# Routing attention with a feed-forward block: one pair's loads ahead of the staging loads, one pair's ordering a step later, and the first result product ahead of the last hidden product

## The chip, the cores and the metric

One core of a Trainium2 chip runs the whole program. Times are device microseconds (us) of one execution; the figure compared is the median over the runs shown. The core's engines work side by side, each on its own queue of instructions: TensorE (PE, matrix products), VectorE (DVE), ScalarE (ACT), GpSimd (POOL) and SyncE (SP). SP does no arithmetic here; it issues nearly all plain DMA transfers. POOL issues the indirect ones.

## The reference

Inputs are random float32. First comes attention by clusters for 4 batches of 8 heads, 768 tokens of 64 features, 16 centroids for each head:

```python
q_assign = np.argmax(np.einsum('bhsd,hcd->bhsc', q_n, c_n), axis=-1)
k_assign = np.argmax(np.einsum('bhsd,hcd->bhsc', k_n, c_n), axis=-1)
mask = q_assign[:, :, :, None] == k_assign[:, :, None, :]
scores = scale * np.matmul(q, k.transpose(0, 1, 3, 2))
scores = np.where(mask, scores, -1000000000.0)
attn = softmax(scores)
x = (attn @ v).transpose(0, 2, 1, 3).reshape(3072, 512)
h = x @ w_in                                       # w_in 512 x 2048
g = np.maximum(h, 0.0) + alpha * np.minimum(h, 0.0)
out = g @ w_out                                    # w_out 2048 x 512
```

(`q_n`, `k_n`, `c_n` are the rows divided by their norms; the softmax is shortened here.) A query meets only the keys that have the same nearest centroid.

## The kernel before, in words

**Pairs and steps.** Two heads of one batch make a pair; there are 16. Pairs 0 to 8 are computed with a mask over all keys. Pairs 9 to 15, the seven ordered pairs, have their tokens sorted by cluster first, so that a block of queries meets only a near window of keys. The program is a hand-written order over 75 steps `u`, of which an ordered pair takes three. Pair 9 starts at step 48 (438.5 us), pair 10 at 51 (461.4), pair 11 at 54 (494.6), pair 8 in two halves at 57 and 60 (517.4, 544.2), pair 12 at 63 (575.9), 13 at 66 (621.4), 14 at 69 (661.4), 15 at 72 (702.9). After step 75 (747) only the feed-forward block of the last batch is left. A step has five slots; small pieces of preparation are listed under (step, slot), and `feed` puts feed-forward pieces of earlier batches between them: first layer L1066 on PE, its copy L1072 on ACT, its slopes L1058 on DVE, second layer L1084 on PE, additions L1090 and L1092, store L1095. Each engine works strictly in the order of its queue. So an instruction that waits holds back whatever stands behind it on that engine.

**How a pair is ordered.** `load(n)` reads q and k (L127). `order_features` transposes them on DVE (L567), `order_sims` multiplies with the centroids on PE (L575), an argmax on DVE follows in pieces (L404 to L412), then a transpose L584 and a scan L589 that counts members. `order_begins` sums counts on PE (L601); `order_ranks` and `order_rows` (L609 to L622) make of it the row to which each token goes. After that 24 indirect DMAs on POOL scatter the tokens into scratch memory (L675). They are fed from staging tiles: `order_stage` (L661) issues three SP loads (q, k, v; "a staging trio" below) into one of two tiles, and waits until the scatters that still read that tile are done. POOL is paced by ACT (L651, L652), so that scatters go out a few to a slot.

**How an ordered pair is loaded and used.** `order_load` (L681 to L708) reads the sorted rows back with 12 SP transfers: two at L688 (where each row came from), eight of 96 KB at L697 (q and k), two at L706 (v). `order_blocks` transposes q and k (two L713 on DVE), `order_queries` makes the query clusters (L719), `score` multiplies (L784; the near windows of the second half bank wait for the first exponential, L802), L825 masks, L835 and L867 add up, L873 and L881 turn and sum for the denominators, L894 folds these sums on PE, and L939 or L972 multiplies with v. Results are put back into token order by indirect transfers (L1011), fetched (L1023) and turned (L1030).

**When these happen.** Two lists of steps set it. `ORDERS` (L1369) gives the step at which `load(n)` of the n-th ordered pair is called; its features come one step later, its sims two. `order_load` is called a number of steps ahead of the pair's start (L1380):

```python
    ORDERS = [26, 29, 35, 38, 41, 56, 59]
    load_at.setdefault(u - (3 if n in (NO + 1, NO + 2, NP - 1) else 4), []).append(
        lambda n=n: order_load(n))
```

Here `u` is the first step of the pair, `NO` is 9 and `NP` is 16: pairs 10, 11 and 15 are loaded three steps ahead, the others four. What is called in `load_at` stands at the head of its step, staging trios and scatters stand in its slots.

**The last batch.** Its feed-forward block (`last_pieces`, L1142) forms 2 x 2 block products with seven multiplications instead of eight, in both layers. `hidden(x)` for x = 0 to 7 makes the products p1, p5, p2, p6, p3, p7 and p4 of the first layer (L1244, two float32 matmuls of 384 columns each); p4 of one x is held in the list `late` and run within the next. p4 is written to the PSUM bank that p7 has used, which DVE reads for an addition (L1179); slopes are at L1184. `final(t)` makes the same seven of the second layer (L1300, one float32 matmul of 256 columns for each of the eight x). For these DVE forms sums of hidden values (`g_sums`, L1223) and of the weights w_out (`w_out_sums`, L1232), four each for every x. `room_for_y` (L1338) stands between the last `hidden` and the first `final`: it runs the held p4 of x = 7, and makes the sums of x = 6 and 7.

Of the kernel before, what the change touches and what calls it, by code (L numbers as in the profile page):

```python
# [16 lines left out]
ALU = mybir.AluOpType  # L17
# [6 lines left out]
def kernel(  # L24
# [80 lines left out]
    NO = WHOLE * NCH - 3  # L105
    NP = len(pairs)
# [4 lines left out]
    def load(n):  # L111

        b, hp = pairs[n]
        for w, src in enumerate((q, k)):
            raw = inp.tile([P, 2, NJ, D], FP32, name="qk")
            if n < NCH:
                nc.sync.dma_start(
                    out=raw.rearrange("p h j d -> p h (j d)"),  # L120
                    in_=src[b, 2 * hp:2 * hp + 2].rearrange("h (p j) d -> p h (j d)",
                                                            j=NJ))
            for h in range(2):
                rows = src[b, 2 * hp + h]
                for x in range(D // Q if n >= NCH else 0):
                    r = h * D + x * Q
                    nc.sync.dma_start(  # L127
                        out=raw.rearrange("p h j d -> p (h j d)")[r:r + Q, :].rearrange(
                            "p (t i) -> p t i", i=Q),
                        in_=rows[:, x * Q:(x + 1) * Q].rearrange("(t p) i -> p t i", p=Q))  # L130
            raw_qk[n, w] = raw
# [306 lines left out]
    def prep_clusters(n):  # L438


        first = firsts.pop(n)
        ps = misc()
        for g in range(NG):
            nc.tensor.matmul(out=ps[:, g * 2 * NX:(g + 1) * 2 * NX], lhsT=spread[:, g, :],
                             rhs=first, start=True, stop=True)
        every = fsp.tile([P, NG, GT, NG, 2], BF16, name="every")
        everys[n] = every
        later(1, lambda: nc.scalar.copy(every.rearrange("p g i r h -> p (g i r h)"),
                                        ps[:, 0:NG * 2 * NX]))
        later(2, lambda: prep_keys(n))  # L450
# [114 lines left out]
    def order_features(n, w):  # L565
        us[n, w] = raw_qk.pop((n, w)).rearrange("p h j d -> p (h j d)")
        nc.vector.transpose(out=us[n, w], in_=us[n, w])  # L567

    def order_sims(n):
        hp = pairs[n][1]  # L570
        ps = misc()
        for g in range(NG):
            w, half = divmod(g, 2)
            tokens = us[n, w].rearrange("p (x g i) -> p g x i", g=2, i=Q)
            nc.tensor.matmul(out=ps[g * W:(g + 1) * W, 0:HS],  # L575
                             lhsT=cT[:, hp * W:(hp + 1) * W], rhs=tokens[:, half],
                             start=True, stop=True)
        later(1, lambda: order_counts(n, ps))
# [131 lines left out]
    def order_blocks(n, w):  # L710
        if w == 0:
            qkTs[n] = qkp.tile([P, NB * P], FP32, name="qkT")
        nc.vector.transpose(  # L713
            out=qkTs[n][:, w * S:(w + 1) * S],
            in_=raw_qk.pop((n, w)).rearrange("p h j d -> p (h j d)"))
# [170 lines left out]
    parts, totals = {}, {}  # L886
# [222 lines left out]
    KH, NQ, HC = NCH // 2, NF // 2, DM // 2  # L1109
# [32 lines left out]
    def last_pieces():  # L1142
# [53 lines left out]
        def g_sum(x, m):  # L1196

            if m == "S4":
                return s4[x]
            t = by_pair[x // 2].rearrange("p (x m q) -> p x m q", x=2, m=2)  # L1200
            return t[:, x % 2, ("S1", "S2").index(m)]
# [8 lines left out]
        def w_out_form(m, x):  # L1210
            if m in ("11", "21", "22"):
                c0 = HC * (m == "22")
                return w_out_sb[:, x if m == "11" else NQ + x, c0:c0 + HC]
            i = ("T1", "T2", "T3", "T4").index(m)
            f = x + NQ * (i // 2)
            return w_in_sb[:, KH * (i % 2):KH * (i % 2 + 1), f * P:(f + 1) * P]

        def g_sums(x):
            (t0, t1), (z0, z1) = g[x][0], g[NQ + x][0]
            S1, S2, S4 = (g_sum(x, m) for m in ("S1", "S2", "S4"))  # L1220
            for to, p, q, op in ((S1, t1, z1, ALU.add), (S2, S1, t0, ALU.subtract),
                                 (t1, t0, t1, ALU.subtract), (S4, z0, S2, ALU.subtract)):
                nc.vector.tensor_tensor(out=to, in0=p, in1=q, op=op)  # L1223

        def w_out_sums(x):

            T1, T2, T3, T4 = (w_out_form(m, x) for m in ("T1", "T2", "T3", "T4"))
            B11, B12, B21, B22 = (
                w_out_sb[:, f, c0:c0 + HC].rearrange("p (a w) -> p a w", a=KH)
                for f in (x, NQ + x) for c0 in (0, HC))  # L1230
            for to, p, q in ((T1, B12, B11), (T2, B22, T1), (T3, B22, B12), (T4, B21, T2)):
                nc.vector.tensor_tensor(out=to, in0=p, in1=q, op=ALU.subtract)  # L1232

        late = deque()
# [101 lines left out]
            return [p1, p5, p6, p2, p7, p3, p4]  # L1336

        def room_for_y():  # L1338
            late.popleft()()
            t = sorts["xmore"].tile([P, NCH, HS], FP32, name="xT").rearrange(  # L1340
                "p c q -> p (c q)")
            ys.extend(ypool.tile([P, DM], FP32, name="y") for _ in range(HJ))
            ys.extend(t[:, i * DM:(i + 1) * DM] for i in range(HJ))
            for x in (NQ - 2, NQ - 1):
                g_sums(x)
            for x in (NQ - 2, NQ - 1):
                w_out_sums(x)
        pieces = []
        for x in range(NQ):
            pieces += hidden(x)  # L1350
        pieces.append(room_for_y)
        for t in range(HJ):
            pieces += final(t)
# [12 lines left out]
    FREE = SLOTS * SB - 3  # L1366


    ORDERS = [26, 29, 35, 38, 41, 56, 59]  # L1369
    prep_at, load_at = {}, {}  # L1370
    for (n, half), u in start_of.items():
        def at(step, slot, piece):
            prep_at.setdefault((step, slot), []).append(piece)
        if half is None:
            t = ORDERS[n - NO]
            load_at.setdefault(t, []).append(lambda n=n: load(n))
            for i in range(2):
                at(t + 1, FIRST + i, lambda n=n, i=i: order_features(n, i))
            at(t + 2, 2, lambda n=n: order_sims(n))
            load_at.setdefault(u - (3 if n in (NO + 1, NO + 2, NP - 1) else 4), []).append(  # L1380
                lambda n=n: order_load(n))
            at(u - 4, 0, lambda n=n: prep_clusters(n))
            for i in range(2):
                at(u - 1, i, lambda n=n, i=i: order_blocks(n, i))
                at(u - 1, FIRST + i, lambda n=n, i=i: order_queries(n, i))
            continue
        if half == 0:
            if n < NCH:
                if n > 1:
                    load_at.setdefault(max(u - 7, 0), []).append(lambda n=n: load(n))  # L1390
                if n > 0:
                    load_at.setdefault(max(u - 6, 0), []).append(lambda n=n: load_v(n))
            else:
                load_at.setdefault(u - 9, []).append(lambda n=n: load(n))
                load_at.setdefault(u - 7, []).append(lambda n=n: load_v(n))
            if n < NCH:
                for g in range(len(groups)):
                    at(u - 4, FIRST + g, lambda n=n, g=g: prep_features(n, g))
            else:
                for w in range(2):  # L1400
                    at(u - 7, FIRST + w + (u - 7 == TOGETHER - 1),
                       lambda n=n, w=w: prep_blocks(n, w))
            at(u - (3 if n < NCH else 5 if u - 6 < TOGETHER else 6), FIRST,
               lambda n=n: prep_sims(n)) if u - 6 < 2 * TOGETHER else at(
                   u - 6, FIRST + 1, lambda n=n: prep_sims(n))
            if n >= NCH:
                at(u - 4, FIRST if u - 4 < TOGETHER else 0, lambda n=n: prep_clusters(n))
        if n < NCH:

            if half == 1 or n == 0:  # L1410
                at(u - (3 if half else 1), FIRST,
                   lambda n=n, half=half: prep_queries(n, half, 0))
            continue
        for h in range(2):
            at(u - 1, FIRST + h, lambda n=n, half=half, h=h: prep_queries(n, half, h))
# [44 lines left out]
    for u in range(-AHEAD, TOGETHER):  # L1460
        for piece in load_at.get(u, []):
            piece()
        n, half, s = steps[max(u, 0)]
# [51 lines left out]
    for u in range(TOGETHER, NS + 1):  # L1515
        for piece in load_at.get(u, []):
            piece()
        if u < NS:
            n, half, s = steps[u]
# [107 lines left out]
    for i in (1, 3):  # L1627
# [14 lines left out]
                            op=ALU.subtract)  # L1642
    nc.vector.tensor_tensor(out=ends[:, 1, :], in0=ends[:, 1, :], in1=spans[:, 2, :],
                            op=ALU.subtract)
# [172 lines left out]
```

## Time and profile before

| | us |
|---|---|
| median of three runs | 940.79 (940.7 to 941.31) |
| profiled execution | 941.51 |
| its span on the core | 939.6 |
| PE busy | 919.1 |
| VectorE busy | 656.2 |
| POOL busy | 382.3 |
| ScalarE busy | 262.8 |

The span runs from the first to the last instruction on the core; the profiled execution's own time lies 1.9 us above it. Busy time is the sum of an engine's instructions, waits not counted. The mean granted clock of PE was 0.997 of full speed. Lines such as L713 are those of the kernel before. In a timeline row the columns are start, duration, engine, line, operation, output and inputs, shapes and count; a bracket at its end gives the time for which the engine stood idle before it, and what ended that. The trace counts two PE instructions for each float32 matmul of the code, and the text counts as the trace does. Rows of one line are joined, so the duration of an "x8" row is from the start of the first to the end of the last, with up to 0.2 us of overlap with its neighbours.

### The profile page before, as it was taken

The page shows a single profiled execution, that of the slowest core. Times are in us where ns is not written, and L with a number is a line of the kernel's source. Part 1 is how long each engine was busy: PE and PEld are TensorE (multiplying, and loading weights), DVE is VectorE, ACT ScalarE, POOL GpSimd, SP SyncE. Part 2 cuts the span into 40 slices and gives each one's busy share as a digit, 9 for nine tenths or more (in the row PEclk, how much of TensorE's full clock was granted, in tenths as well). Part 3 has the DMA queues.
Part 4 walks back from the last instruction along what each step waited for, and adds up shares of the span by engine and source line. Part 5 has one row for each costly group of instructions (what it writes and reads, how often), then busy time and mean ns, then how long its engine had stood idle before and what let it go on. Part 6 is the DMA issues. An engine that isn't in the chain of part 4 may idle for free.

```text
span 939.6 us, 11988 instructions
## 1 busy us (share of the span) xinstructions
PE 919.1 (98%) x3963; PEld 495.3 (53%) x3963; DVE 656.2 (70%) x1246; ACT 262.8 (28%) x661; POOL 382.3 (41%) x580
## 2 busy tenths in 40 slices
PE   8999999999999999999999999999999999999997
PEld 5534444445455454454544544555555555556886
DVE  5797798799679589598987889754647135598100
ACT  5764444323023132231212332122212120221000
POOL 2333222200026677478575786668533471000000
PEclk9999999999999999999999999999999999999999
DMA  8433758039002635252952383662501012000000
GB/s 298 135 117 98 144 131 150 18 62 196 1 9 72 156 82 137 62 120 76 176 100 41 59 138 73 149 124 60 92 31 27 12 37 53 1 0 1 23 23 25
DMA packets 226708, 77.71 MB, mean 83 GB/s; under 512 B 210752, under 2 KB 214544, under 8 KB 226640
## 3 DMA queue, kind: packets, MB, share of 16 engines
q1 hardware_dynamic: 217728, 62.72, 30.9%
q0 software_dynamic: 8064, 13.78, 4.7%
q8 instruction: 33, 0.54, 0.2%
q10 hardware_dynamic: 848, 0.39, 0.2%
q14 instruction: 35, 0.29, 0.1%
HBM read 52.25 MB, written 24.25 MB: 81 GB/s over the span
## 4 chain that ended last, share of the span: by engine, by line
PE 82%; DVE 10%; SPq 3%; DMA 1%; issue 1%; POOL 1%; ACT 1%; DVEq 0%; POOLq 0%; ACTq 0%
PE fps L1084 24%; PE fps L1066 22%; PE sps L784 6%; PE vps L939 5%; PE sps L1244 4%; PE sps L1300 4%; PE vps L1244 2%; PE vps L1300 2%; PE fps L784 2%; SPq L697 1%; PE mps L972 1%; PE fps L1300 1%; PE fps L1244 1%; PE vps L972 1%; SPq L127 1%
## 5 line engine op out<-in xcount | busy, mean ns | idle before, releaser
L1066 PE MATMUL fps<-xT,w_in_sb 128*128 128x384 f32 x768 | 258.9, 490 | 0.0
L1084 PE MATMUL fps<-w_out_sb,gT 128*128 128x512 f32 x576 | 254.8, 596 | 2.5 <-DVE gT L1058 2.5
L675 POOL DMA_INDIRECT scratch<-stage,off x168 | 177.9, 1059 | 75.1 <-issue 29.6
L1066 PEld LDWEIGHTS fps<-xT,w_in_sb 128*128 128x128 f32 x768 | 142.5, 190 | 103.1 <-issue 4.3
L1084 PEld LDWEIGHTS fps<-w_out_sb,gT 128*128 128x128 f32 x576 | 107.4, 190 | 134.8 <-issue 121.4
L1072 ACT COPY gT<-fps 128x384 f32<-128x384 f32 x96 | 46.0, 479 | 236.2 <-PE fps L1066 236.2
L652 POOL COPY paced<-pace 1x1 f32<-1x1 f32 x205 | 51.2, 250 | 139.5 <-ACT pace L651 138.9
L1058 DVE SCALAR_TENSOR_TENSOR gT<-gT,alpha 128x384 f32<-128x384 f32 x96 | 61.2, 647 | 58.7 <-ACT gT L1072 58.5
L1011 POOL DMA_INDIRECT back<-rows,off x84 | 85.7, 1021 | 24.2 <-issue 18.6
L784 PE MATMUL sps<-qkT 64*128 64x384 f32 (+1 forms) x464 | 86.1, 490 | 0.4 <-DVE qkT L713 0.4
L805 ACT ACTIVATE E<-sps 128x768 f32<-128x768 f32 (+1 forms) x76 | 56.3, 786 | 62.6 <-PE sps L793 38.4
L784 PEld LDWEIGHTS sps<-qkT 64*128 64x128 f32 x464 | 41.8, 188 | 39.7 <-issue 14.6
L825 DVE SCALAR_TENSOR_TENSOR more<-aq,key,more 128x384 f32<-128x384 bf16 (+2 forms) x116 | 60.4, 577 | 0.0
L939 PE MATMUL vps<-E,vt 128*64 128x384 f32 x292 | 54.2, 495 | 1.5 <-DVE xT L1042 1.5
L271 POOL TENSOR_TENSOR w_in_sb<-w_in_sb,power 128x512 f32<-128x512 f32 x16 | 25.7, 1612 | 68.6 <-DVE w_in_sb L268 68.6
L825 DVE SCALAR_TENSOR_TENSOR E<-aq,key,E 128x384 f32<-128x384 bf16 (+2 forms) x88 | 45.3, 569 | 0.6 <-ACT E L802 0.6
L271 POOL TENSOR_TENSOR w_out_sb<-w_out_sb,power 128x512 f32<-128x512 f32 x16 | 22.5, 1412 | 56.0 <-DVE w_out_sb L268 56.0
L907 DVE RECIPROCAL inverses<-mps 64x12 f32<-64x12 f32 (+1 forms) x42 | 10.5, 249 | 48.1 <-PE mps L894 47.9
L835 DVE TENSOR_TENSOR acc<-acc,E 128x768 f32<-128x768 f32 x35 | 33.3, 951 | 14.6 <-ACT E L805 13.6
L1090 ACT COPY y<-fps 128x512 f32<-128x512 f32 x18 | 10.6, 587 | 102.3 <-PE fps L1084 102.3
L1092 DVE TENSOR_TENSOR y<-y,fps 128x512 f32<-128x512 f32 x24 | 16.3, 680 | 28.5 <-PE fps L1084 28.5
L805 ACT ACTIVATE more<-sps 128x768 f32<-128x768 f32 (+1 forms) x40 | 29.2, 764 | 12.5 <-PE sps L784 11.6
(284 smaller groups left out, 1178.4 us busy)
## 6 DMA issues: line engine op xcount, KB each, us to landing
raw<-in_moe_w_in_dram SPq DMA_DIRECT2D x16, 512.0 KB
raw<-in_moe_w_out_dram SPq DMA_DIRECT2D x16, 512.0 KB
out_dram<-y SPq DMA_DIRECT2D x21, 256.0 KB
qk<-scratch SPq DMA_DIRECT2D x56, 96.0 KB
qk<-in_q_dram SPq DMA_DIRECT2D x48, 96.0 KB
qk<-in_k_dram SPq DMA_DIRECT2D x48, 96.0 KB
w_in_kept<-w_in_sb SPq DMA_DIRECT2D x8, 512.0 KB
vt<-in_v_dram SPq DMA_DIRECT2D x9, 384.0 KB
```

The lines of the kernel that those rows point to most:

```text
L652: nc.gpsimd.tensor_copy(out=sorts["paced"], in_=token)
L675: nc.gpsimd.indirect_dma_start(out=scratch[n][1][h * NX + xx], out_offset=bass.IndirectOffsetOnAxis(ap=ranks[n][:, xx, h:h + 1], axis=0), ...
L784: nc.tensor.matmul(out=bank(ps, h, m), lhsT=qkT[r:r + D, S + c * P:S + (c + 1) * P], rhs=qkT[r:r + D, tokens], start=True, stop=not early_ ...
L805: nc.scalar.activation(out=E[:, :, 0:m], in_=ps[:, :, 0:m], func=AF.Exp, scale=SCALE)
L825: nc.vector.scalar_tensor_tensor(out=e, in0=of, scalar=keys[n][:, NJ + c, h:h + 1], in1=e, op0=ALU.is_equal, op1=ALU.mult)
L939: nc.tensor.matmul(out=po[r:r + D, 0:HS], lhsT=vts[n][:, h, c, :], rhs=e[:, h, :], start=(c == 0), stop=(c == NJ - 1))
L1011: nc.gpsimd.indirect_dma_start(out=to[i], out_offset=bass.IndirectOffsetOnAxis(ap=place[:, h, j:j + 1], axis=0), in_=rows[j // HJ][:, j % ...
L1058: nc.vector.scalar_tensor_tensor(out=gs[f], in0=gs[f], scalar=alpha[:, f:f + 1], in1=gs[f], op0=ALU.mult, op1=ALU.max)
L1066: nc.tensor.matmul(out=ps[:, 0:HS], lhsT=w_in_sb[:, c, f * P:(f + 1) * P], rhs=xTs[b, half][:, c, :], start=(c == 0), stop=(c == NCH - 1))
L1084: nc.tensor.matmul(out=ps[:, 0:DM], lhsT=gs[f][:, i * P:(i + 1) * P], rhs=w_out_sb[:, f, :], start=on and f == f0, stop=off and f == f0 + ...
L1244: nc.tensor.matmul(out=bank[to], lhsT=w_in_form(m, x, cc), rhs=rhs[:, cc, :], start=start and cc == 0, stop=cc == KH - 1, skip_group_check ...
L1300: nc.tensor.matmul(out=bank[to], lhsT=g_form(m, x, t), rhs=w_out_form(n, x), start=start and x == 0, stop=x == NQ - 1, skip_group_check=no ...
```

## The change

Three edits. First, the leads of `order_load` become a list, in which pair 11 has 4 steps instead of 3: its loads are called at step 50, not 51. All other leads keep their value. Second, the last entry of `ORDERS` is 60, not 59: loading, ordering, staging and scattering of pair 15 start one step later. Third, `room_for_y` no longer runs the held p4 of x = 7 and no longer makes the sums itself. It appends them to `late`, as eight pieces: piece i of x = 6, then piece i of x = 7, for i = 0 to 3, each with one sum of hidden values and one of weights. `late` is emptied in p1 of `final(0)`, which was there before: p1 is issued first, then p4 of x = 7, then the sums.

```diff
-        def g_sums(x):
+        def g_sums(x, parts=range(4)):
             (t0, t1), (z0, z1) = g[x][0], g[NQ + x][0]
             S1, S2, S4 = (g_sum(x, m) for m in ("S1", "S2", "S4"))
-            for to, p, q, op in ((S1, t1, z1, ALU.add), (S2, S1, t0, ALU.subtract),
-                                 (t1, t0, t1, ALU.subtract), (S4, z0, S2, ALU.subtract)):
+            sums = ((S1, t1, z1, ALU.add), (S2, S1, t0, ALU.subtract),
+                    (t1, t0, t1, ALU.subtract), (S4, z0, S2, ALU.subtract))
+            for to, p, q, op in [sums[i] for i in parts]:
                 nc.vector.tensor_tensor(out=to, in0=p, in1=q, op=op)
 
-        def w_out_sums(x):
+        def w_out_sums(x, parts=range(4)):
...
-            for to, p, q in ((T1, B12, B11), (T2, B22, T1), (T3, B22, B12), (T4, B21, T2)):
+            sums = ((T1, B12, B11), (T2, B22, T1), (T3, B22, B12), (T4, B21, T2))
+            for to, p, q in [sums[i] for i in parts]:
                 nc.vector.tensor_tensor(out=to, in0=p, in1=q, op=ALU.subtract)
...
         def room_for_y():
-            late.popleft()()
...
-            for x in (NQ - 2, NQ - 1):
-                g_sums(x)
-            for x in (NQ - 2, NQ - 1):
-                w_out_sums(x)
+            late.extend(lambda i=i, x=x: (g_sums(x, [i]), w_out_sums(x, [i]))
+                        for i in range(4) for x in (NQ - 2, NQ - 1))
...
-    ORDERS = [26, 29, 35, 38, 41, 56, 59]
+    ORDERS = [26, 29, 35, 38, 41, 56, 60]
+    LEADS = [4, 3, 4, 4, 4, 4, 3]
...
-            load_at.setdefault(u - (3 if n in (NO + 1, NO + 2, NP - 1) else 4), []).append(
+            load_at.setdefault(u - LEADS[n - NO], []).append(
                 lambda n=n: order_load(n))
```

## The prediction, made before the result was known

> **What bounds the kernel now.** First the engine totals. TensorE (PE) is busy for 919.1 of 939.6 us and no other engine is above 70%, so time can be won only where PE waits or runs slowly.
>
> ```profile
> span 939.6 us, 11988 instructions
> PE 919.1 (98%) x3963; PEld 495.3 (53%) x3963; DVE 656.2 (70%) x1246; ACT 262.8 (28%) x661; POOL 382.3 (41%) x580
> ```
>
> Second, the waits of PE over the whole run. A row is: waiting line, releaser, us in total, times, longest. Those the change can reach:
>
> ```profile
> PE fps L1084 <- DVE gT L1058: 2.5, 2, 2.3
> PE mps L575 <- issue: 1.3, 1, 1.3
> PE mps L601 <- DVE simT L589: 1.1, 2, 0.8
> PE fps L784 <- ACT E L802: 0.7, 1, 0.7
> PE sps L1244 <- DVE gT L1179: 0.6, 1, 0.6
> PE sps L784 <- DVE qkT L713: 0.4, 1, 0.4
> ```
>
> Third, the chain of waits around the largest of them, at 490 us. A row is start, duration, what:
>
> ```profile
> 486.40 3.60 DMA qk<-scratch
> ...
> 490.13 0.98 DVE qkT L713
> ...
> 491.53 0.54 DVE gT L1058
> ...
> 492.11 2.59 PE fps L1084 x4
> 494.70 2.26 PE sps L784 x8
> ```
>
> PE waits for a slope (L1058). The slope stands on VectorE (DVE) behind the second transpose L713 of pair 11, and that one waits for the last load of pair 11. Fourth, the timeline of SyncE's queue (SP) shows why the load is late (start, us, instruction):
>
> ```profile
> 466.33 0.39 SPq L141 DMA_DIRECT2D vt<-in_v_dram  x1
> 472.92 0.61 SPq L661 DMA_DIRECT2D stage<-in_q_dram  x1
> ...
> 479.09 0.60 SPq L661 DMA_DIRECT2D stage<-in_q_dram  x1
> ...
> 482.36 4.61 SPq L697 DMA_DIRECT2D qk<-scratch  x8
> ```
>
> SP stood still twice, 466.7 to 472.92 and 474.95 to 479.09, in front of a staging load that waits for the scatters still reading its tile. The loads L697 stood behind both. Last, windows of 1 us over PE (busy, busy with count, granted clock, DMA share, GB/s):
>
> ```profile
> 491.00:492.00 1.00, 0.00 (x0) 1.00 0.00 0
> ...
> 494.00:495.00 1.00, 1.00 (x3) 0.50 0.00 0
> ...
> 497.00:498.00 1.00, 1.00 (x8) 1.00 0.12 33
> ```
>
> The clock was halved from about 493.3 to 496.8. So the wait costs more than its 2.29 us.
>
> **What the Trainium skill says.** "TensorE: Matmul & The Clock Gate", Part 1: the clock has two values, full and half; it drops after an idle window of about 3.4 us and comes back after about as long of work. The trace agrees on one half and on the length (493.3 to 496.8), but here an idle of 2.29 us was enough, while PE's other idles of 1.0 to 1.5 us show no drop; the trace decides. "DMA: Bandwidth & Descriptors", section on the anatomy of one DMA: transfers wait on nothing, the issuing sequencer does, before it dispatches. SP's two stops above are that, so the place in SP's order is what matters. "PSUM — Partial Sum Buffer", section on bank collisions: PE must not write a bank while it is read. This is the 0.65 us wait of part C.
>
> **Part A: pair 11's load one step earlier (step 51 to 50).** In the built program its 12 DMAs (2 at L688, 8 at L697, 2 at L706) now stand directly behind the store L1095 of 465.68, ahead of L141 and both staging trios. They can go: the last scatter of pair 11 was issued at 414.91, and the buffer's last reader, pair 10's second L713, ended near 460. They issue over 466.3 to 473.4 (7.1 us, the old length from 481.06 to 488.4), 15 us earlier. DVE's order is the same. Its first L713 lost 1.44 us and its second 1.80 us to these loads. Without them DVE starts the first at 485.85 and runs two L713 at 0.98, L455, L459 (0.4 together) and the first slope (0.5) to about 488.65. PE ends its 12 matmuls L1084 at 489.82 and finds the slope ready, 1.2 us early. So the wait of 2.29 goes. So does the halved clock: x4 of L1084 take 1.72 instead of 2.59 (a group of 16 takes 6.87 undisturbed), and the 8 score matmuls L784 take 1.29 instead of 2.26 (same form at 461.40 and 575.94). The fold L894 then starts at 489.82+1.72+1.29+0.54 = 493.4 instead of 497.5: **4.1 us**.
> What is pushed back: L141 and the first trio by about 1 us (SP is done with the loads at 473.4, the trio began at 472.92); the second trio still waits for its scatters until about 479.1. The scatters fed by them may come 1 to 2 us later; the scatter queue (POOL) later has 6.63 us of wait for its pace at 495.54, which covers this. DMA load between 466 and 472 is light (44 to 55 GB/s).
>
> **Part B: ordering of pair 15 one step later (59 to 60).** What moves: on SP the four-plus-four loads L127 (548.90 to 554.5) go behind a staging trio; on DVE two L567, then the argmax (L404 to L412), L584, L589 and ranks; on PE the sims L575 and the begins L601; on SP and POOL pair 15's staging trios and scatters.
>
> ```profile
> 560.35 1.07 PE L575 MATMUL mps<-qk,cT 128*32 128x384 f32 x8 [1.34 <-issue]
> 575.94 1.29 PE L784 MATMUL sps<-qkT 64*128 64x224 f32 x8 [0.40 <-DVE qkT L713]
> 578.47 0.80 PE L784 MATMUL fps<-qkT 64*128 64x320 f32 x2 [0.71 <-ACT E L802]
> 586.22 0.58 PE L601 MATMUL mps<-simT,row 128*128 128x1 f32 x4 [0.83 <-DVE simT L589]
> ```
>
> L575 waits for the second L567, which waited 2.23 and 0.33 us for its loads. In the built order L575 stands in the middle of the second group of L1084, about 569 us; L567 can be done at about 565.6: 1.34 goes. Pair 12's second L713 no longer has L404, L405 and L406 of pair 15 in front of it (some 1.7 us of DVE): done about 571.7, wanted at 574.0: 0.40 goes. L601 stands behind 8 L1084 and 12 L1066, its scan has 8 us more: 0.83 goes. The 0.71 stays: it is the second half bank waiting for the first exponential, in both programs. Sum **2.57 us**. Thin place: L404 now stands in front of the parts that the fold L894 of pair 12 needs, behind a transpose L1030 that may wait for a fetch; worked out, 576.4 against 577.2 wanted, 0.8 us to spare. Bounds for B: below, -1 us (that margin overrun, nothing else gained in this stretch); above, 3.3 (the 0.71 goes too). Later price: pair 15's order_load, issued from 657.01 to 663.9 and landed by about 666, now comes about one step later, 13 us (pair 13 to pair 14 is 40 us for three steps), while PE is 6.7 earlier by then. Pair 15's first L713 starts at about 692, so of 26 us of slack some 6 are left: cost nothing, but less cover than before.
>
> **Part C: first product of the results ahead of the last of the first layer.** Nothing is added or removed; DVE has as many sums as before.
>
> ```profile
> 857.81 1.45 PE L1244 MATMUL sps<-xT,w_in_sb 128*128 128x384 f32 x4
> 859.91 1.56 PE L1244 MATMUL sps<-vt,w_in_sb 128*128 128x384 f32 x4 [0.65 <-DVE gT L1179]
> 868.22 3.77 PE L1300 MATMUL vps<-w_in_sb,qkT 128*128 128x256 f32 x16
> ```
>
> Product p4 waits for the addition of p7 (859.30 + 0.56), which reads p4's bank. After: p7 ends 859.26, p1 takes 3.45 in between, p4 1.29, then p2, p5, p6 at 3.45 each: 874.35, where before the product after p6 began at 875.27. Gain **0.9 us** (0.65, the 0.12 by which p4 ran long, and 0.15 in p5, whose sums came late). Needed: p1's slopes (done 860.37, wanted by 862.3), the slopes behind p4 (865.1, wanted 867.0), the first sums interleaved (867.7, wanted 870.5). Bounds: 0 if a sum in the new order is late by as much, 1.2 at most.
>
> **Sum.** 4.1 + 2.57 + 0.9 = 7.6 us. The profiled execution took 941.51 (span 939.6 and 1.9 around it), so 933.9; the median of the runs is 940.79, 0.72 lower, so **933.2**. From 730 to 857 PE has no wait that takes any of it back; between 595 and 730 the gaps that remain belong to PE's own order.
>
> **Rivals.** (1) A and C hold, B does not: DVE is the bound of the stretch from 560 to 590 (it is busy there without a gap), and L404 ahead of the fold's input turns the 0.8 us margin into a wait of the size removed. For it: a thin margin, and L1030 waiting on a fetch. Against: 2 us of argmax work leave the place. 940.79 - 5.0 = 935.8. (2) B and C hold, A does not: the slope has to wait for something else, such as a delayed load or a later staging trio, and PE idles again at 490. Against: the loads have 15 us. About 937.3 with the clock drop kept. (3) The wait goes but the halved clock turns up at another place, since the window that decides it runs freely; 2 of 7.6 us are clock: 935.5. (4) Nothing measurable, the next late input stands right behind each: 940 to 941. (5) Slower: pair 15's later staging. Its 24 scatters go out at the pace that ScalarE sets; if order_load(15) slips, L713 at step 71 and the score at step 72 wait, 1 us for each, plus 1.8 us of halved clock. It decides from a slip of some 12 us beyond the 13 worked out: 6 to use up the slack, about 6 more and the 1.8 to lose the gain. 941 to 946.
>
> **How the numbers follow.** All parts hold: 0.68, with 931 to 935 (clock and small idles). Rival 1: 0.11; rival 2: 0.08; rival 3: 0.05; rival 4: 0.04; rival 5: 0.04. The range 931 to 938 takes in the first four. A measurement here tells 0.2% (1.9 us) from no change; faster by more is 0.92, within it 0.04, slower 0.04.
>
> **What would show it.** In the changed profile: the L697 of pair 11 at 466 to 473; no wait at L1084 near 490 and clock 1.00 from 490 to 500; no wait at L575 and L601 of pair 15 nor at the score of pair 12, the 0.71 kept; the 0.65 at L1244 gone and p5 at 3.45; span near 932.0. Wrong would be a new PE wait near 577 at L894 (B), near 488 at L1084 (A), at step 72 on L784 for L713 (rival 5), or half-clock slices elsewhere.

## The result, and the profile after

| | before | after |
|---|---|---|
| median, six runs each | 941.12 us | 934.10 us |
| ratio of the runs | | 0.9928, 95% interval 0.9918 to 0.9937 |
| profiled execution | 941.51 | 933.59 |
| its span | 939.6 | 931.8 |
| PE busy | 919.1 | 916.7 |

The changed kernel is faster by 0.72%, about 6.8 us; the interval allows 5.9 to 7.7. Beside later experiments it was run once more (`changed_again` below): 934.62, ratio 0.9926.

In the changed kernel lines up to L1179 keep their numbers; L1223, L1232, L1244 and L1300 of before are now L1224, L1234, L1246 and L1302. The page of after, and from its list of PE's waits the rows that answer to those shown of before:

```profile
span 931.8 us, 11987 instructions
PE 916.7 (98%) x3963; PEld 495.0 (53%) x3963; DVE 655.9 (70%) x1246; ACT 263.9 (28%) x662; POOL 384.9 (41%) x581
```

```profile
PE mps L972 <- DVE inverses L907: 1.2, 1, 1.2
PE mps L575 <- ACT rows L1005: 1.1, 1, 1.1
PE fps L784 <- ACT E L802: 0.7, 1, 0.7
PE mps L601 <- DVE simT L589: 0.3, 1, 0.3
PE fps L1084 <- DVE gT L1058: 0.3, 1, 0.3
```

What is missing counts: the 2.29 us at L1084, the 1.34 at L575, the 0.83 at L601, the 0.40 at L784 and the 0.65 in the last first-layer product. The waits that remain were there before too; the one at L972 is a little longer (1.16 against 0.90), but in other traces with the new order of loads it lies anywhere from 0.6 to 1.4. PE's busy sum fell by 2.4 us though it does the same matmuls: part of them had run at half clock.

SyncE's timeline of after (start, us, instruction), and windows of 1 us over PE:

```profile
466.76 1.12 SPq L688 DMA_DIRECT2D off<-scratch  x2
467.99 6.35 SPq L697 DMA_DIRECT2D qk<-scratch  x8
474.43 1.13 SPq L706 DMA_DIRECT2D vt<-scratch  x2
475.66 0.50 SPq L141 DMA_DIRECT2D vt<-in_v_dram  x1
476.35 1.36 SPq L661 DMA_DIRECT2D stage<-in_q_dram  x1
```

```profile
491.00:492.00 1.00, 1.00 (x4) 1.00 0.12 33
494.00:495.00 1.00, 1.00 (x9) 1.00 0.00 0
```

Pair 11's loads issue in front of both stops, and where PE stood idle at 491 and ran at 0.50 at 494 it is now busy at 1.00. For the other two parts, PE's timeline:

```profile
565.76 0.85 PE L575 MATMUL mps<-qk,cT 128*32 128x384 f32 x8
...
570.17 1.29 PE L784 MATMUL sps<-qkT 64*128 64x224 f32 x8
...
572.70 0.80 PE L784 MATMUL fps<-qkT 64*128 64x320 f32 x2 [0.71 <-ACT E L802]
573.44 0.40 PE L894 MATMUL mps<-part,fold 128*128 128x24 f32 x2
...
851.28 1.45 PE L1246 MATMUL sps<-xT,w_in_sb 128*128 128x384 f32 x4
...
856.02 1.45 PE L1246 MATMUL sps<-vt,w_in_sb 128*128 128x384 f32 x4
...
860.76 3.62 PE L1302 MATMUL vps<-w_in_sb,qkT 128*128 128x256 f32 x16
```

Neither the sims of pair 15 nor pair 12's score has a bracket any more; the second half bank keeps its 0.71. p7 starts at 851.28, and p4 (856.02) now follows p1 without a wait.

Landmarks on PE, by which the 7.8 us between the two spans can be split (up to the first of them the two executions do the same, so its -0.27 is the spread between executions):

| landmark | before | after | gained so far | by this stretch |
|---|---|---|---|---|
| score of pair 10 starts | 461.40 | 461.67 | -0.27 | -0.27 |
| fold L894 behind pair 11's score | 497.43 | 493.76 | 3.67 | 3.94 (A) |
| p7 of x = 7 starts | 857.81 | 851.28 | 6.53 | 2.86 (B) |
| next product after p6 starts | 875.27 | 867.67 | 7.60 | 1.07 (C) |
| end of the span | 939.6 | 931.8 | 7.8 | 0.2 |

### The profile page after: what moved, and what is told of

Same layout as the page of the kernel before. It is cut to its first block, busy times and chain, and to the rows that moved or that the text cites. A ratio compares the mean times of both kernels' runs of the same rounds, so it can differ in the third digit from the quotient of the medians.

```text
span 931.8 us, 11987 instructions
## 1 busy us (share of the span) xinstructions
PE 916.7 (98%) x3963; PEld 495.0 (53%) x3963; DVE 655.9 (70%) x1246; ACT 263.9 (28%) x662; POOL 384.9 (41%) x581
## 4 chain that ended last, share of the span: by engine, by line
PE 89%; DVE 5%; SPq 2%; issue 1%; DMA 1%; POOL 1%; ACT 1%; DVEq 0%; POOLq 0%; ACTq 0%
PE fps L1084 26%; PE fps L1066 25%; PE sps L784 7%; PE vps L939 6%; PE sps L1302 4%; PE sps L1246 4%; PE fps L784 2%; PE vps L1246 2%; PE vps L1302 2%; PE mps L972 1%; PE fps L1302 1%; PE fps L1246 1%; PE vps L972 1%; PE sps L793 1%; PE mps L383 1%
## 5 line engine op out<-in xcount | busy, mean ns | idle before, releaser
L1084 PE MATMUL fps<-w_out_sb,gT 128*128 128x512 f32 x576 | 254.2, 595 | 0.3 <-DVE gT L1058 0.3
L1084 PEld LDWEIGHTS fps<-w_out_sb,gT 128*128 128x128 f32 x576 | 107.5, 190 | 132.2 <-issue 121.6
L652 POOL COPY paced<-pace 1x1 f32<-1x1 f32 x206 | 54.2, 263 | 115.5 <-ACT pace L651 115.0
L784 PE MATMUL sps<-qkT 64*128 64x384 f32 (+1 forms) x464 | 85.0, 485 | 0.0
L784 PEld LDWEIGHTS sps<-qkT 64*128 64x128 f32 x464 | 41.2, 186 | 38.6 <-issue 14.8
L651 ACT COPY pace<-ones 1x1 f32<-1x1 f32 x206 | 29.5, 185 | 31.6 <-POOL paced L652 31.5
```

The lines of the kernel that those rows point to most:

```text
L652: nc.gpsimd.tensor_copy(out=sorts["paced"], in_=token)
L784: nc.tensor.matmul(out=bank(ps, h, m), lhsT=qkT[r:r + D, S + c * P:S + (c + 1) * P], rhs=qkT[r:r + D, tokens], start=True, stop=not early_ ...
L1084: nc.tensor.matmul(out=ps[:, 0:DM], lhsT=gs[f][:, i * P:(i + 1) * P], rhs=w_out_sb[:, f, :], start=on and f == f0, stop=off and f == f0 + ...
```

## The experiments

Each kernel below ran beside the kernel before on the same chip; the median of that stands with it.

**Each edit by itself.**

```diff
only_a, against the kernel before
-            load_at.setdefault(u - (3 if n in (NO + 1, NO + 2, NP - 1) else 4), []).append(
+            load_at.setdefault(u - (3 if n in (NO + 1, NP - 1) else 4), []).append(
only_b, against the kernel before
-    ORDERS = [26, 29, 35, 38, 41, 56, 59]
+    ORDERS = [26, 29, 35, 38, 41, 56, 60]
only_c, against the changed kernel
-    ORDERS = [26, 29, 35, 38, 41, 56, 60]
-    LEADS = [4, 3, 4, 4, 4, 4, 3]
+    ORDERS = [26, 29, 35, 38, 41, 56, 59]
+    LEADS = [4, 3, 3, 4, 4, 4, 3]
```

> Pair 11's loads one step earlier, the other two edits undone. Theory (the loads were the late input, and the wait of 2.29 us drags a halved clock of 1.8 us behind it): 4.1 us below the kernel before, about 937.0 of 941.1; no wait at L1084 near 490 and a clock of 1.00 there. Rival (the halved clock falls in the profiled execution alone): about 2.3 us below in the timed runs. Rival (the time is lost again to the scatters and staging pushed back): less than 1 us below, with a new wait of PE after 497.

> Pair 15 ordered one step later, the other two edits undone. Theory: the waits of 1.34, 0.40 and 0.83 us go, 0.71 stays: 2.6 us below, about 938.5. Rival (VectorE bounds 560 to 590 and the argmax in front of the fold gives the waits back): within 0.5 us of the kernel before, with a new wait of PE at L894 or L939 near 577. Here order_load of pair 15 comes about 13 us later with only some 2.6 us of PE gained before it, so the slack before L713 of pair 15 should be 9 to 11 us.

> First product of the results ahead of the last hidden product, with the sums interleaved, the other two edits undone. Theory: the wait of 0.65 us and the 0.3 us beside it go: 0.9 to 1.1 us below, about 940.1; from the start of p7 to the end of p6 16.4 us where it was 17.5. Rival: the sums now come late for p5 and give it back: no difference, and a wait of PE at the second layer.

| | median | before | ratio, 95% interval |
|---|---|---|---|
| only_a | 937.9 | 941.61 | 0.9955 (0.9941 to 0.9969) |
| only_b | 938.79 | 941.61 | 0.9967 (0.9955 to 0.9979) |
| only_c | 940.8 | 941.61 | 0.9992 (0.9983 to 1.0001) |

The differences of the medians are 3.7, 2.8 and 0.8 us, 7.3 together: the three edits add up, within their intervals, to what they do at once. PE's timeline in only_a:

```profile
485.25 7.03 PE L1084 MATMUL fps<-w_out_sb,gT 128*128 128x512 f32 x16
...
493.98 0.42 PE L894 MATMUL mps<-parts,fold 128*128 128x48 f32 x2
```

PE has no wait within L1084, starts the fold at 493.98 and runs at 1.00 from 491 to 496. In only_b the waits of 1.34, 0.40 and 0.83 us are gone and PE's wait for the slope near 490 is still 2.2. In only_c p7 starts at 858.12 and the product after p6 at 874.52: 16.40 us, where the kernel before took 17.46; its time alone could not tell 0.8 us from nothing, the trace does. One expectation of only_b missed: the slack in front of pair 15's L713. order_load is issued at 677.06 and L713 starts at 691.53, 14.5 us apart, against 36 before (657.01 to 692.97); with some 9 us for issue and landing (657.01 to about 666, the prediction's figure) about 5.5 are left, not 9 to 11.

**Which of SyncE's two stops made the loads late.** `order_load(11)` is called within step 50 instead of at its head:

```diff
between_stops, against the changed kernel
+            if n == NO + 2:
+                at(u - 4, 2, lambda n=n: order_load(n))
+            else:
+                load_at.setdefault(u - LEADS[n - NO], []).append(
+                    lambda n=n: order_load(n))
```

> The changed kernel, with pair 11's loads put behind L141 and the first staging trio, ahead of the second trio: SyncE's first stop is in front of them, its second behind. Theory (only the second stop made them late): they issue from about 475 to 482, land near 485, the two L713 start at 486.3 with no wait, and the time is that of the changed kernel within 0.2%; no wait of PE near 490. Rival (the first stop counts too): a wait of 1 us or more at L713 and of PE at L1084 near 490.

934.01 us (before 941.65), ratio 0.9919 (0.9901 to 0.9937). SyncE's timeline, and VectorE's:

```profile
474.58 0.61 SPq L661 DMA_DIRECT2D stage<-in_q_dram  x1
...
477.85 5.12 SPq L697 DMA_DIRECT2D qk<-scratch  x8
```

```profile
487.34 1.83 DVE L713 STREAM_TRANSPOSE qkT<-qk 128x768 f32<-128x768 f32 x2
```

The first stop (up to 474.58) is still in front of the loads. They issue at 477.85, the two L713 start at 487.34 back to back with no wait, and PE waits nowhere near 490. The 15 us by which the edit moves the loads are more than was needed: to take the loads out from behind the second stop is enough.

**Moving p4 without the new order of the sums.**

```diff
sums_in_old_order, against the changed kernel
-            late.extend(lambda i=i, x=x: (g_sums(x, [i]), w_out_sums(x, [i]))
-                        for i in range(4) for x in (NQ - 2, NQ - 1))
+            late.extend(lambda of=of, x=x: of(x)
+                        for of in (g_sums, w_out_sums) for x in (NQ - 2, NQ - 1))
```

> The changed kernel with p4 behind p1, but the sums of x = 6 and 7 in their old order (all four of hidden values of 6, of 7, then the weights of 6, of 7). Theory (moving p4 is worth the gain only because the sums come in the order in which p5 and p6 need them): p5 needs the first weight sum of x = 6 at about 863.4 and of x = 7 at 863.8, and gets them near 863.2 and 864.6: a wait of 0.7 to 0.9 us inside p5, so 0.8 us above the changed kernel, all of part C gone. Rival (the move alone carries it): the same as the changed kernel within 0.2 us, no wait there.

936.22 us (before 941.61), ratio 0.9942 (0.9928 to 0.9955), against 0.9926 and 0.9928 of the changed kernel. PE's timeline in p5:

```profile
861.53 3.50 PE L1302 MATMUL vps<-w_in_sb,qkT 128*128 128x256 f32 x14
...
864.33 0.70 PE L1302 MATMUL vps<-w_in_sb,qkT 128*128 128x256 f32 x2
865.79 0.70 PE L1302 MATMUL vps<-w_in_sb,qkT 128*128 128x256 f32 x2 [0.77 <-DVE w_in_sb L1234]
```

The row at 864.33, from a narrower window, is the last pair of the x14. VectorE's timeline has the two sums:

```profile
863.85 0.42 DVE L1234 TENSOR_TENSOR w_in_sb<-w_out_sb 128x256 f32<-128x256 f32 x1
...
865.32 0.42 DVE L1234 TENSOR_TENSOR w_in_sb<-w_out_sb 128x256 f32<-128x256 f32 x1
```

The last two matmuls of p5 wait 0.77 us for the weight sum T1 of x = 7 (done 865.74), as worked out. The two in front of them are late as well, by 0.21 us: they start at 864.33, when T1 of x = 6 is done (864.27), where twelve matmuls at 0.216 us from 861.53 end at 864.12. The expectation had that sum in time. From p7 to the product after p6 it is 17.74 us: more than before the change. So the move of p4 needs the new order of the sums; alone it only moves the wait. (The new order without the move was not tried.) The cost is 1.34 us (17.74 less 16.40) for both waits: see the last section.

**Part B: one cause or several.** Ordering at the old step, but pair 15's q and k read a step earlier:

```diff
early_load, against the changed kernel
-    ORDERS = [26, 29, 35, 38, 41, 56, 60]
+    ORDERS = [26, 29, 35, 38, 41, 56, 59]
-            load_at.setdefault(t, []).append(lambda n=n: load(n))
+            load_at.setdefault(t - (n == NP - 1), []).append(lambda n=n: load(n))
```

> The changed kernel with pair 15 ordered at the old step (59), but its q and k read one step earlier, ahead of the staging trios of that step. Theory (part B's three waits have two causes: late loads make the 1.34 us, the place of the argmax and of L601 in the queues makes 0.40 and 0.83): the wait at L575 goes, the 0.40 at L784 and 0.83 at L601 stay, 1.2 us above the changed kernel, about 935.6. Rival (one cause, the late loads): all three go, as in the changed kernel. Rival (VectorE's order makes the first too): all three stay, 2.6 us above it.

938.24 us (before 941.65), ratio 0.9968 (0.9957 to 0.998). The theory fell: all three waits went, as the first rival had it, so the 0.40 and the 0.83 were followers of the late loads (VectorE had lost 2.23 and 0.33 us to them at L567), not of the place of the argmax. But the kernel is no match for the changed one. SyncE's timeline, VectorE's and PE's:

```profile
531.82 2.92 SPq L127 DMA_DIRECT2D qk<-in_k_dram  x4
```

```profile
542.05 1.04 DVE L1030 STREAM_TRANSPOSE xT<-qk 128x384 f32<-128x384 f32 x2 [1.18 <-DMA qk<-back]
```

```profile
550.70 0.58 PE L601 MATMUL mps<-simT,row 128*128 128x1 f32 x4 [1.60 <-DVE simT L589]
```

The early loads stand on SyncE from 517 to 531.8 with no buffer to go to (its waits are 5.9 us for a transpose L567 and 8.9 us for the sims L575 of the pair before, which still use the buffers), and hold back a staging trio and the fetch L1023 behind them (537.09, in the changed kernel 534.99). The turn L1030 waits for that, the scan L589 of pair 14 stands behind L1030 on VectorE, and PE waits for the scan, 1.60 us where the changed kernel waits 0.31. That is 1.3 us of the 4.1 by which the medians differ. In the profiled run, the fastest at 936.14, the mean clock was 0.999; in the six others (937.77 to 939.07) it was 0.997 or 0.998. The four traces with a halved stretch among the matmuls (before, only_b, only_c, two_more) all have 0.997, the others 0.998 or more. So most of the slower runs probably had such a stretch; after which wait is not shown, and the rest of the 4.1 us stays open.

**Rival 5, pushed a step further.**

```diff
order_61, against the changed kernel
-    ORDERS = [26, 29, 35, 38, 41, 56, 60]
-    LEADS = [4, 3, 4, 4, 4, 4, 3]
+    ORDERS = [26, 29, 35, 38, 41, 56, 61]
+    LEADS = [4, 3, 4, 4, 4, 4, 2]
```

> The changed kernel with pair 15 ordered yet one step later (61), its order_load therefore two steps ahead of its start. Its last scatter comes about 13 us later, near 683, and its loads land near 693, where the changed kernel starts L713 of pair 15 at 686.4. Theory as the prediction had it (slack ends where L713 is due, each us beyond it costs one): L713 is 5 to 7 us late, PE waits as long and runs 1.8 us at half clock, 940 to 943. Rival (the changed kernel's trace: between L713 and the score at 696.4 PE has only first-layer products to do, which need no slope, so some 8 us more can slip): L713 waits 4 to 7 us and PE nothing or less than 1 us, 934 to 935.

934.37 us (before 941.65), ratio 0.9927 (0.9914 to 0.9939): no slower than the changed kernel. Both expectations of the loads were wrong. SyncE's and VectorE's timelines:

```profile
678.38 0.95 SPq L688 DMA_DIRECT2D off<-scratch  x2
```

```profile
687.38 1.83 DVE L713 STREAM_TRANSPOSE qkT<-qk 128x768 f32<-128x768 f32 x2
```

order_load came 6.4 us later (678.38 against 671.95), not 13, and L713 did not wait. The slack is about used up, though: the last L697 is issued at 684.1, and with the 3.2 us to landing that are the median of these loads in the changed kernel, an estimate for its landing is 687.3. In GpSimd's timeline of the changed kernel these scatters alternate with the put-backs of earlier results; that their end therefore moves by less than their start is likely, but was not tried by itself. What a real overrun there costs was not tried either.

**Two more moves of the same kind.** Pair 8's loads a step earlier, pair 14's sims a slot later; then the same with pair 11's turn L1030 two slots later, and that turn by itself.

```diff
two_more, against the changed kernel
-            at(t + 2, 2, lambda n=n: order_sims(n))
+            at(t + 2, 3 if n == NP - 2 else 2, lambda n=n: order_sims(n))
-                load_at.setdefault(u - 9, []).append(lambda n=n: load(n))
+                load_at.setdefault(u - (10 if n == NO - 1 else 9), []).append(lambda n=n: load(n))
turn_later, against the changed kernel, and two_more_turn_later, against two_more
-        later(4 if n == NP - 1 else 7, turn_back)
+        later(4 if n == NP - 1 else 9 if n == NO + 2 else 7, turn_back)
```

> The changed kernel and two further moves of the same kind: pair 8's loads one step earlier (L366 waits 0.97 and 0.23 us for them on VectorE, and L907 behind it makes PE wait 1.16 us at L972 near 466), and pair 14's sims L575 one slot later (it waits 1.06 us for the copy L1005 that empties its PSUM tile, and its L601 0.31 us for the scan). If each wait goes and nothing else comes late: 2.2 to 2.5 us below the changed kernel, about 931.8. If VectorE's work behind them is the bound: same as the changed kernel, with the waits at L972 or L601 in other places.

936.82 us (before 941.65), ratio 0.9952 (0.9937 to 0.9968): slower than the changed kernel. The wait at L972 near 466 and the 0.31 at L601 went, the one at L575 stayed (PE's order kept L575 in its place), and a new one came. The chain of waits:

```profile
569.10 3.15 DMA qk<-back
...
572.38 1.04 DVE xT L1030 x2
573.41 0.48 DVE simT L404
...
573.93 0.40 PE mps L894 x2
```

```profile
573.93 0.40 PE L894 MATMUL mps<-part,fold 128*128 128x24 f32 x2 [2.46 <-DVE simT L404]
```

PE stands 2.46 us in front of L894, because L404, which empties the PSUM tile that the fold writes, waits behind L1030, and L1030 waits 4.21 us for a fetch. After it the windows show the clock at 0.50 from 575 to 577. This is the thin place that the prediction named in part B, overrun.

> The changed kernel once more, beside the two below: 934.1, 0.992 to 0.993 of the kernel before.

> The changed kernel with pair 11's turn L1030 two slots later, behind L404, L719, L405 and L1092 on VectorE, so that its wait for the fetch no longer stands in front of the copy L404 that frees the tile of the fold L894. Theory (in the changed kernel L404 ends 0.6 us before L894 wants it, so nothing waits yet): same as the changed kernel within 0.2%, L404 ends about 570 instead of 572.8. Rival (L1030's 1.75 us of VectorE idle already costs PE later): 0.5 to 1.5 us below it.

> Both further moves (pair 8's loads a step earlier, pair 14's sims a slot later) together with the later turn L1030. Theory (two_more lost because PE reached the fold L894 2.4 us before L404 was through, L404 standing behind L1030 and its 4.2 us wait for the fetch): the wait of 2.46 us at L894 and the halved clock behind it go, and the 2.2 to 2.5 us of the two moves are kept: about 931.8, 2.3 below the changed kernel. Rival (VectorE is late there for another reason, or L1030 now holds up L907 and the masks): a wait of 1 us or more at L939, L784 or L894 between 570 and 585, and no better than the changed kernel.

| | median | ratio, 95% interval (before 941.34) |
|---|---|---|
| changed_again | 934.62 | 0.9926 (0.9911 to 0.9941) |
| turn_later | 934.22 | 0.9924 (0.9909 to 0.9939) |
| two_more_turn_later | 933.0 | 0.9908 (0.9893 to 0.9923) |

VectorE's timeline of the last:

```profile
569.04 0.54 DVE L404 STREAM_TRANSPOSE simT<-mps 128x384 f32<-128x384 f32 x1
...
573.21 1.04 DVE L1030 STREAM_TRANSPOSE xT<-qk 128x384 f32<-128x384 f32 x2 [1.74 <-DMA qk<-back]
```

L404 is through at 569.6, long before PE wants the fold (572.38), and L1030's wait now costs nothing. So the later turn is worth nothing to the changed kernel, and some 4 us once PE comes earlier (ratios 0.9952 and 0.9908). two_more_turn_later has the lowest median of all; against the changed kernel beside it that is 1.6 us. The intervals of the ratios overlap, but the six runs of the one (931.75 to 933.34) all lie below the six of the other (933.75 to 934.95), and the two waits missing from its trace (1.16 and 0.31 us) are of that size. The 2.2 to 2.5 expected counted the wait at L575, which did not move.

## Why the prediction held

**Part A.** The loads, the vanished wait and the vanished half clock are as worked out. From the start of the L1084 group to L894 before took 12.92 us (484.51 to 497.43) and after 8.73 (485.03 to 493.76): 4.19, where 4.1 was predicted; only_a's trace has 8.73 too. The timed runs of only_a gained 3.7, with an interval of 2.9 to 5.6 that takes in 4.1. If 3.7 is right, the term most likely too large is the halved clock, taken as 1.8 us in every execution. Of 41 runs of the kernel before beside the experiments 19 had a mean clock of 0.997 or less, like the traces with a halved stretch, and a mean time of 942.0; 13 had 0.999 or more, and 940.5; their traces were not kept. The other 9, at 0.998, can be either: sums_in_old_order has 0.998 without a halved stretch among its matmuls, since the clock falls after the last one too, where it costs nothing. So the 1.8 us fell due, by this estimate, in 19 to 28 of the 41: 2.3 + 0.46 x 1.8 to 2.3 + 0.68 x 1.8, or 3.1 to 3.5.

What stood beside it was read less well, without harm. DMA was not light where the loads went: before, it moved 217 to 273 GB/s from 467 to 470. The 12 loads took 8.8 us of SyncE (466.76 to 475.56), not 7.1, and the first trio came 3.4 us later (476.35 against 472.92), not about 1. No wait of PE came of it.

**Part B.** 2.57 predicted, 2.86 in the trace, 2.8 in the runs. The sum was right. The reading of it as three waits with three reasons was not needed: early_load, with the argmax and L601 in their old places, took away all three by earlier loads alone. Rival 1 (VectorE bounds the stretch) fell: once its waits for loads are gone it keeps up. Its margin at L404 was real: predicted 0.8 us, in after L404 ends at 572.80 and L894 starts at 573.44, 0.64.

```profile
571.30 1.04 DVE L1030 STREAM_TRANSPOSE xT<-qk 128x384 f32<-128x384 f32 x2 [1.75 <-DMA qk<-back]
572.26 0.54 DVE L404 STREAM_TRANSPOSE simT<-mps 128x384 f32<-128x384 f32 x1
```

The slack of pair 15 came out near the 6 us predicted, by a wrong route. The distance from order_load to L713 shrank from 36.0 to 14.5 us both in only_b, where L713 comes 1.4 us earlier than before (691.53 against 692.97), and in the changed kernel, where it comes 6.5 earlier (686.44). So the 21.5 us are the price of the step itself, not 13 and PE's gain added. That the predicted 6 us came out is luck: the step was taken as 8.5 us too cheap, and PE's 6.7 us were counted against it though they cost nothing.

**Part C.** 0.92 predicted, 1.07 measured: 0.92 at p4, where 0.65 and 0.12 had been counted, and 0.14 in p5. That the sums must be interleaved was in the list of what was needed, and sums_in_old_order showed that without it the part brings nothing: 17.74 us where the kernel before took 17.46.

**Sum.** 7.6 was predicted, and the two profiled executions differ by 7.92 (941.51 to 933.59). The ratio of the runs gives 6.8, with 7.6 still inside its interval (5.9 to 7.7). The forecast of 933.2 is 0.9 below the measured 934.1: 0.3 of it because three more runs put the median of the kernel before at 941.12 and not 940.79, and the clock term that is not due in every execution is large enough (0.6 to 1.0 by the estimate above) for the rest. Rivals 2, 3 and 4 show in no view: no wait at 490, and no window of 1 us before 930 with a clock below 1.00.

## What to carry to other kernels

When one queue issues both transfers that must wait for a buffer and transfers that are ready, place the ready ones ahead; ask what stands at the head of the queue, not how long a transfer takes. Before pulling a load still earlier, ask where it would land: with no buffer free it becomes the stop it was meant to pass. After a gain, look for the next wait that is hidden by less than the gain; here 1.5 us of removed waits became a loss of about 2 us, until one instruction was put ahead of a waiting turn.

## What the runs showed of the hardware

**When the clock halves.** The traces record each change of TensorE's clock. Before, it is full for 488.11 us, half for 3.41, full for 440.32; in the changed kernel full for 925.01. All such stretches, in all 13 traces, are (but for the last, cut off by the end) whole multiples of 3.413 us (these: 143, 1, 129 and 271). So the clock changes only at the borders of intervals of 3.413 us, and where the borders lie differs from one execution to the next. Put windows on these intervals, and the rule shows (before; only_b; only_c twice; two_more):

```profile
489.94:493.35 3.41, 1.24 (x3) 1.00 0.27 53
493.35:496.76 3.41, 3.41 (x10) 0.50 0.00 0
491.40:494.81 3.41, 1.29 (x3) 1.00 0.29 57
494.81:498.22 3.41, 3.41 (x12) 0.50 0.00 0
489.28:492.69 3.41, 1.25 (x4) 1.00 0.53 102
492.69:496.10 3.41, 3.41 (x10) 0.50 0.00 0
557.55:560.96 3.41, 1.71 (x10) 1.00 0.17 43
560.96:564.37 3.41, 3.41 (x15) 1.00 0.17 53
570.87:574.29 3.42, 0.96 (x6) 1.00 0.50 106
574.29:577.70 3.41, 3.41 (x13) 0.50 0.22 63
```

In the 13 traces every interval with 2.12 us of idle or more was followed by one at half clock: these four, and in each trace the one in which the idle behind the last matmul first reached 2.18 us or more. None with 1.70 or less was; what lies between was not seen. It is the idle within one interval that counts, not the length of the wait. That would explain why the same wait of 2.29 us halves the clock in some executions only: a border that falls into it splits it. If the borders fall anywhere with equal chance, an estimate is that 2.12 us of it lie within one interval in 43 of 100 executions and 1.70 us in 68; the 19 to 28 of 41 runs are 46 to 68 of 100. No trace was kept of an execution that has the wait and no drop, so this last step is not shown. The same wait can thus cost 2.3 or some 4 us from one execution to the next, and a single profile tells only one of the two.

**What a wait costs.** A wait of PE costs more than the idle time shown for it. Matmuls of 256 columns follow each other every 0.216 us (3.46 from the start of the 16 at 860.76 to the next product), but a lone pair shows 0.59, and the pair after the wait in sums_in_old_order 0.70: the idle is counted from the modelled end of the last, and the overlap with the next is lost on top. There the pair in front, late itself, starts at 864.33. If it can be followed after 0.54 us, as the pair behind the wait is (865.79 to 866.33; without a wait it is 0.43), that pair comes 0.92 late and costs 0.11 more: 1.03 for an idle of 0.77. In part C an idle of 0.65 cost 0.92 (3.50 from p7's start to the first product behind p4, where two undisturbed products of 1.29 are 2.58).
